# Fourier mixing with a gated convolution: the order of the first 55 microseconds changed on GpSimd, VectorE, ScalarE and TensorE

## The chip, the cores and the metric

The kernel runs on one core of a Trainium2 chip. A core has five engines with a queue of instructions each: TensorE (PE; its weight loads are PEld), VectorE (DVE), ScalarE (ACT), GpSimd (POOL) and SyncE (SP), which only starts transfers here. Within a queue the order is fixed when the program is built; between queues, semaphores carry the dependences. The metric is the time of one execution on the device, in microseconds.

## The reference

For each of 8 batches, `x` has 3136 positions and 256 features, all float32.

```python
X = np.fft.fft(x, axis=1); X = np.fft.fft(X, axis=2); x = X.real
h = np.maximum(x @ w_in, 0.0)                     # w_in 256 x 1024
conv_out[s] = conv_w[0]*h[s-1] + conv_w[1]*h[s] + conv_w[2]*h[s+1]   # zeros at both ends
out = (h * (1/(1+exp(-conv_out)))) @ w_out        # w_out 1024 x 256
```

The weights come as float64, each value in two 32-bit words, and have to be made float32 on the chip.

## The kernel before, in words

**Stages.** The transform along the sequence is folded by symmetry. Rows `x[s]` and `x[S-s]` are added and subtracted on VectorE (`xh`, then `w`), and TensorE multiplies the parts with tables of cosines and sines (`tab_109`, `tab_110`, 98 or 99 rows). This gives the two halves of the spectrum, `pt` and `qt`, in nine *units* for a batch: odd and even ones for both halves, and one called `feature`, which makes a single edge row (`pd`, then `er`). A unit has matmuls into a PSUM tile `po`, a `copy` of half of it to `as` on ScalarE, and a `fin` of sums and differences on VectorE that writes `pt` or `qt`. `part(0)` and `part(1)` are the two parts of an odd unit's matmuls. The tables are mirrored at run time on ScalarE (`mirror_even`, `mirror_tables`), and `mend_row` halves one row of them there.

The transform along the features is folded into the weights: TensorE multiplies `w_in` with a small table `dm` to give `G` (`blocks`, copied by ScalarE) and a column sum `ge` (`column`). So `w_in` has to be float32 first. It is converted in four quarters of two feature blocks each, `w_in[0]` to `w_in[3]`. Each of `w_in[1]` to `w_in[3]` takes five operations of VectorE and one of ScalarE: exponent (L653), a power of two from it (ScalarE, L655), mantissa (L667), lower word added (L668), sign (L661), product (L676). `w_out` follows by the same way.

**The main loop.** A batch is cut along the sequence in 4 *chunks*, each with 8 feature blocks of 128, which makes 32 *steps* a batch and 256 in all. Step s goes through these stages, at the cycles of the loop named in brackets, relative to its own: `seed` (ScalarE puts `eb` times `ge` in `pa`; -2), `products` (TensorE, into `pb` and `pa`; -1), `copies` (ScalarE, `nb` out of `pb`; -1), `combine` (VectorE, two custom instructions, `h` out of `pa` and `nb` with the relu; 0), `first_tap` (ScalarE, `g`; 0), `middle` (a transfer that adds the shifted `h` to `g`, started by GpSimd; 0), `last_tap` (VectorE; +3), `sigmoid` (ScalarE) and `gate` (VectorE; +4), and the product with `w_out` (TensorE; +5).

`row_of` takes an `h` tile for a step and has GpSimd set its two end columns to zero where the chunk asks for it (L820); `combine` of the step waits for that. In cycle t it is called for step t+1, ahead of `middle(t)`.

**What sets the order.** No scheduler: instructions stand on each queue in the order of the code. The loop has named places ("first", "act", "dve", "pool", "load", "pe"), and `at(cycle, place, f)` hangs extra work on one of them. With that the head of the program hands on what it has not done: the rest of the weights' conversion, `column` and `blocks` of the later quarters, and the loads for the next batch.

**The edge row.** `feature` writes the even entries of `er` on GpSimd (L459, L460). `flip` fetches the odd ones from the last partition of `qt` by a transfer on SP (L488), and GpSimd then negates every second of these (L489, the *sign change*). `store` writes `er` to a buffer in memory (`ed`, L492), and `spread` loads it back over all partitions, one tile `eb` for each chunk (L595). The first chunk's `eb` is not made in that way but in PSUM (`odd_first`, `even_first`, L981).

Of the kernel before, what the change touches and what calls it, by code (L numbers as in the profile page):

```python
# [10 lines left out]
I32 = mybir.dt.int32  # L11
U32 = mybir.dt.uint32
AF = mybir.ActivationFunctionType
# [24 lines left out]
def kernel(  # L38
# [100 lines left out]
    def fold_ops(b):  # L139
# [4 lines left out]
        def half(h):  # L144
# [65 lines left out]
            def scaled():  # L210
                if b == 0 and h:
                    a, c = sides()
                    for i, (v, k) in enumerate(((a, 0), (c, 2), (a, 1), (c, 0))):
                        if i % 2 == 0:
                            parted[h, i // 2] = hp.tile([P, HW], F32, name="h", tag="h")[:, 0:4 * P].rearrange(
                                "p (a s d) -> p a s d", a=2, s=2)
                        act(parted[h, i // 2][0:NP, i % 2], v, AF.Copy, scale=turn[0:NP, k, h:h + 1])
                    return
                made.append(rp.tile([P, 2, 2, P], F32, name="rt", tag="rt"))
                for i, v in enumerate(sides()):  # L220
                    act(made[0][0:NP, i], v, AF.Copy, scale=turn[0:NP, 1, h:h + 1])
# [84 lines left out]

    def mend_row(par, half):

        for st in range(2):
            row = tabs[0][96:NP, st, HQ - 1] if par == 0 else tabs[1][96:NP, st, 1]  # L310
            act(row, row, AF.Copy, scale=half[96:NP])

    def mirror_tables(h):

# [36 lines left out]
    def units(b):  # L351
# [134 lines left out]
        def flip():  # L486

            nc.sync.dma_start(out=er[b][:, 1:NK:2], in_=PQ[b][1][P - 1:P, 1:NK:2])  # L488
            nc.gpsimd.tensor_scalar(out=er[b][:, 3:NK:4], in0=er[b][:, 3:NK:4], scalar1=-1.0, scalar2=None, op0=ALU.mult)  # L489

        def store():
            nc.sync.dma_start(out=ed[b:b + 1, 0:NK], in_=er[b])  # L492

        return (begin, [odd_even(1), odd(1), even_even(1), even(1), feature(), odd_even(0), odd(0),
# [144 lines left out]
    def narrow(dst, raw, room=None):  # L639
# [7 lines left out]
        if room is not None:  # L647
            c, n = hi.shape[1:]
            sg = room[:, 0:c * n].rearrange("p (c n) -> p c n", c=c)

        def power():

            ts(out=d, in0=hi, scalar1=20, scalar2=0x7FF, op0=lsr, op1=ALU.bitwise_and)  # L653
            if room is not None:
                act(d, d, AF.Relu, scale=2.0 ** 23, bias=low[0:d.shape[0]])  # L655
            else:
                ts(out=d, in0=d, scalar1=-896, scalar2=0, op0=ALU.add, op1=ALU.max)
                ts(out=d, in0=d, scalar1=23, scalar2=None, op0=lsl)
# [1 line left out]
        def sign():  # L660
            stt(out=d, in0=hi, scalar=-0x80000000, in1=d, op0=ALU.bitwise_and, op1=ALU.bitwise_or)  # L661

        def product():

            if room is None:
                sign()
            ts(out=sg, in0=hi, scalar1=0xFFFFF, scalar2=0x100000, op0=ALU.bitwise_and, op1=ALU.bitwise_or)  # L667
            stt(out=lof, in0=lo.bitcast(U32), scalar=2.0 ** -32, in1=sg, op0=ALU.mult, op1=ALU.add)  # L668
            if room is None:
                value()  # L670

        def value():

            if room is not None:
                sign()
            stt(out=dst, in0=lof, scalar=2.0 ** -20, in1=dst, op0=ALU.mult, op1=ALU.mult)  # L676
        return (power, product) if room is None else (power, product, value)

    class Weight:

# [269 lines left out]
    mirror_tables(0)  # L950
    column(0)
    keep_on(1)
    mirror_even(0)
    mend_row(1, half)
    mirror_tables(1)
    folds(1)
    mirror_even(2)
    mend_row(0, half)
    mirror_even(1)
    mirror_even(3)  # L960
    room = left[:, NF // 2:].rearrange("p f i -> p (f i)").bitcast(I32)
    for f in load_ops(1, 0, nc.sync):
        f()
    for u in odds:
        u.part(0)
    for j, u in enumerate(odds):
        u.part(1)
        u.copy()
        u.fin()

    n = chunks[0].k1
    for i, u in enumerate(us[j] for j in (4, 2, 3, 7, 8)):
        u.matmuls(0, 1)
        if i == 0:
            p = spare()
            odd_first(p, n)
        u.copy()
        if i == 2:
            even_first(p, n)
            eb[0, 0] = ebp.tile([P, HN], F32, name="eb", tag="eb")[:, 0:n]  # L980
            nc.scalar.copy(out=eb[0, 0], in_=p[:, 0:n])  # L981
        u.fin()
    flip()
    store()
    spread(0, range(1, len(chunks)))
    steps = [(b, c, f) for b in range(B) for c in range(len(chunks)) for f in range(NF)]
    per = len(chunks) * NF
    side = {}
    taken = set()

# [2 lines left out]

    for i in (2, 3):
        at((0, 0, 1, 3)[i], "pe", lambda i=i: blocks(i))

    early, *rest = w_in[2].parts(0, 2, room)
    at(0, "first", lambda: column(1))
    at(0, "first", lambda: blocks(1))
    for fn in rest:  # L1000
        at(0, "dve", fn)
    for cycle, w_, c in ((1, w_in[3], 0), (3, w_out, 0), (5, w_out, 2), (7, w_out, 4), (9, w_out, 6)):
        for j, where, fn in zip((0, 0, 1), ("first", "dve", "dve"), w_.parts(c, c + 2, room)):
            at(cycle + j, where, fn)
    taken.update((0, 2, 4, 6, 8, 10))
    for j, fn in enumerate(load_ops(1, 1, nc.sync)):
# [67 lines left out]

    LAG = 5
    n = len(steps)
    row_of(steps[0])
    seed(steps[0])
    seed(steps[1])
    products(steps[0])  # L1080
    copies(steps[0])
    for f in w_in[1].parts(0, 2, room):
        f()
    early()
    for t in range(n + LAG):
        def run(where):
            for fn in side.get((t, where), []):
# [19 lines left out]
            last_tap(steps[t - 3])  # L1107
        if 0 <= t - 4 < n:
            gate(steps[t - 4])
        if t + 1 < n:  # L1110
            row_of(steps[t + 1])
        if t < n:
            middle(steps[t])
# [71 lines left out]
```

## Time and profile before

| what | us |
|---|---|
| median of 3 runs | 1160.87 |
| lowest and highest | 1160.75, 1161.49 |
| profiled execution | 1162.03 |
| its span | 1160.3 |
| PE busy in it | 1137.6 |
| DVE busy | 960.4 |
| ACT busy | 902.1 |
| POOL busy | 375.8 |

The granted clock of TensorE is 1.000 over the span. The span is what the trace covers; the rest of the execution lies around it. Times in the rows of the trace are microseconds from the start of the span. In a row there stand the start, the duration, the engine, the line of the kernel, the operation, the tile written and the tiles read, the shape, how many instructions the row groups, and in brackets the idle time of the engine ahead of it with what ended that. [...] PE is near full over the whole span, but not in the first 60 us, and it is these that the change touches.

### The profile page before, as it was taken

How to read it: one execution, taken by the hardware profiler on the slowest of the kernel's cores; microseconds unless marked ns; L12 is line 12 of the kernel's file. 1: busy time of each engine (PE TensorE's matmuls, PEld its weight loads, DVE VectorE, ACT ScalarE, POOL GpSimd, SP SyncE). 2: the span in 40 equal slices, each digit the busy share in tenths (PEclk: the TensorE clock that was granted, in tenths of full speed). 3: DMA queues.
4: the chain of work that ended last, by engine and by line, in shares of the span. 5: the costliest groups of instructions: out<-in, count | busy, mean ns of one | idle time of the engine just before them, and what ended most of it. 6: DMA issues, size and time to landing. Idle time of an engine off the chain costs nothing.

```text
span 1160.3 us, 15073 instructions
## 1 busy us (share of the span) xinstructions
PE 1137.6 (98%) x4824; PEld 887.2 (76%) x4824; DVE 960.4 (83%) x1452; ACT 902.1 (78%) x1709; POOL 375.8 (32%) x484
## 2 busy tenths in 40 slices
PE   6899999999999999999999999999999999999998
PEld 3667787778777877777777777778778777777777
DVE  8799889988988989798878879788886767877775
ACT  3688877878777878787877778887877777888884
POOL 6335523542343252425132331422121222122223
PEclk9999999999999999999999999999999999999999
DMA  9777985876757586756776766765664656666664
GB/s 251 162 109 178 169 159 125 182 167 152 164 120 168 119 198 143 169 114 154 147 171 128 153 140 122 177 129 120 142 128 93 125 118 138 139 131 129 123 118 100
DMA packets 107595, 167.49 MB, mean 144 GB/s; under 512 B 32104, under 2 KB 62838, under 8 KB 107517
## 3 DMA queue, kind: packets, MB, share of 16 engines
q0 software_dynamic: 42160, 115.87, 51.8%
q1 hardware_dynamic: 64616, 50.53, 15.8%
q8 instruction: 38, 0.62, 0.2%
q14 instruction: 40, 0.33, 0.1%
q10 hardware_dynamic: 741, 0.14, 0.1%
HBM read 37.80 MB, written 25.74 MB: 55 GB/s over the span
## 4 chain that ended last, share of the span: by engine, by line
PE 84%; DVE 5%; ACT 4%; issue 2%; POOL 1%; ACTq 0%; POOLq 0%; DVEq 0%
PE po L93 52%; PE pb L93 13%; PE pa L93 13%; PE pd L93 6%; DVE g L858 1%; ACT nb L835 1%; DVE g L885 1%; ACT os L913 1%; DVE h L843 1%; POOL xh L129 1%; ACT g L877 1%; ACT pa L814 0%; ACT g L849 0%; POOL w L176 0%; POOL g L853 0%
## 5 line engine op out<-in xcount | busy, mean ns | idle before, releaser
L93 PE MATMUL po<-wout,g 128*128 128x256 f32 x3072 | 706.3, 379 | 3.3 <-DVE g L885 3.2
L93 PEld LDWEIGHTS po<-wout,g 128*128 128x128 f32 x3072 | 580.6, 190 | 148.0 <-issue 17.6
L853 POOL DMA_DIRECT2D g<-h x256 | 219.7, 858 | 725.3 <-ACT g L849 453.1
L835 ACT ACTIVATE nb<-pb 128x386 f32<-128x386 f32 (+3 forms) x512 | 227.6, 499 | 167.4 <-PE pb L93 166.7
L843 DVE CUSTOM_DVE_ANT_0 h<-pa,nb 128x386 f32<-128x386 f32 (+3 forms) x512 | 265.0, 558 | 35.4 <-PE pa L93 22.6
L877 ACT ACTIVATE g<-g,cw 128x770 f32<-128x770 f32 (+3 forms) x264 | 246.1, 935 | 45.8 <-DVE g L858 44.4
L858 DVE SCALAR_TENSOR_TENSOR g<-h,cw,g 128x770 f32<-128x770 f32 (+1 forms) x256 | 265.4, 1037 | 0.3 <-DMA g<-h 0.3
L885 DVE TENSOR_TENSOR g<-g,h 128x770 f32<-128x770 f32 (+1 forms) x248 | 240.2, 968 | 22.4 <-ACT g L877 22.1
L849 ACT ACTIVATE g<-h,cw 128x770 f32<-128x770 f32 (+1 forms) x256 | 244.1, 953 | 0.0
L93 PE MATMUL pb<-qt,G 127*128 127x387 f32 (+2 forms) x512 | 213.8, 498 | 1.5 <-ACT nb L835 1.1
L93 PE MATMUL pa<-pt,G 128*128 128x387 f32 (+2 forms) x512 | 212.2, 495 | 1.4 <-ACT pa L814 1.3
L814 ACT ACTIVATE pa<-eb,ge 128x387 f32<-128x387 f32 (+2 forms) x256 | 155.3, 607 | 3.1 <-DVE h L843 1.4
L93 PEld LDWEIGHTS pa<-pt,G 128*128 128x128 f32 x512 | 96.5, 189 | 76.6 <-issue 19.2
L129 POOL DMA_INDIRECT xh<-in_x_dram,idx x64 | 97.7, 1527 | 20.2 <-issue 12.7
L93 PE MATMUL pd<-tab,w 98*128 98x197 f32 (+2 forms) x448 | 97.6, 317 | 0.0
L93 PEld LDWEIGHTS pb<-qt,G 127*128 127x128 f32 x512 | 90.9, 190 | 8.5 <-ACT nb L835 2.9
L93 PEld LDWEIGHTS pd<-tab,w 98*128 98x128 f32 (+1 forms) x448 | 82.0, 191 | 8.9
L913 ACT COPY os<-po 128x256 f32<-128x256 f32 x196 | 57.4, 392 | 6.3 <-PE po L93 6.3
L399 DVE TENSOR_TENSOR as<-as,pd 128x196 f32<-128x196 f32 x14 | 5.0, 358 | 46.0 <-ACT as L395 46.0
L176 POOL COPY w<-xh 98x4 f32<-98x4 f32 (+1 forms) x30 | 37.5, 1252 | 7.9 <-DVE xh L170 7.9
L154 DVE TENSOR_TENSOR xh<-xh 98x1020 f32<-98x1020 f32 (+1 forms) x32 | 38.6, 1210 | 0.4 <-DMA xh<-in_x_dram,idx 0.4
L165 DVE TENSOR_TENSOR xh<-xh 98x1024 f32<-98x1024 f32 (+1 forms) x32 | 38.9, 1214 | 0.1
(150 smaller groups left out, 430.4 us busy)
## 6 DMA issues: line engine op xcount, KB each, us to landing
g<-h POOLq DMA_DIRECT2D x192, 385.0 KB, 3.9
g<-h POOLq DMA_DIRECT2D x64, 416.0 KB, 4.2
out_dram<-os SPq DMA_DIRECT2D x96, 256.0 KB
xh<-in_x_dram SPq DMA_DIRECT2D x16, 784.0 KB
eb<-ed SPq DMA_DIRECT2D x16, 193.5 KB
raw<-in_moe_w_in_dram SPq DMA_DIRECT2D x4, 512.0 KB
raw<-in_moe_w_out_dram SPq DMA_DIRECT2D x1, 2048.0 KB
eb<-ed SPq DMA_DIRECT2D x8, 209.0 KB
```

The source lines that it names most:

```text
L93: nc.tensor.matmul(o, l, r, start=start, stop=stop, skip_group_check=True)
L129: nc.gpsimd.indirect_dma_start(out=xh[b, h][0:NP, 7 - m].rearrange("p q d -> p (q d)"), out_offset=None, in_=bass.AP(tensor=x.tensor, offs ...
L165: vt(flat(to, to + 2), flat(0, 2), flat(2, 4), op=op)
L814: act(pa[s][:, 0:n], eb[b, c], AF.Copy, scale=ge[:, f:f + 1])
L835: act(nb[s][:, i, cols], p[:, cols], AF.Copy, scale=-1.0 if i else 1.0)
L843: nc.vector._custom_dve(TENSOR_ADD_SAT, out=to, in0=a[:, cols], in1=c[:, i, cols], s0=BIG, s1=0.0)
L849: act(gs[s], hs[s][:, 0:n], AF.Copy, scale=cw[:, 0, s[2]:s[2] + 1])
L853: nc.gpsimd.dma_start(out=gs[s], in_=hs[s][:, 1:1 + n], accum_op=ALU.add)
L858: stt(out=g, in0=h[:, k:k + n], scalar=cw[:, k, f:f + 1], in1=g, op0=ALU.mult, op1=ALU.add)
L877: act(gs[s][:, c], gs[s][:, c], AF.Sigmoid, scale=cw[:, 1, s[2]:s[2] + 1])
L885: vt(g, g, h[:, 0:r.stop], op=ALU.mult)
L913: nc.scalar.copy(out=osb[:, j % 2], in_=pt[:, j % 2])
```

## The change

The change has three parts.

1. *Memsets and sign change.* `row_of` of steps 0 and 1 is called ahead of the loop, and in the loop for step t+1 from t = 1 on. The sign change moves out of `flip` into `store`, and `store` is hung on cycle 0's place "pool", behind `middle(0)`, with `spread` behind it. `flip`'s transfer is issued after the third of the last five units.
2. *Narrowing of `w_in[1]`.* `parts` gives six operations instead of two or three groups. For `w_in[1]` they are called apart: exponent and mantissa after the odd units, power after the copy of the first `eb`, lower after the third of the last five units, sign and value right ahead of the loop. The other quarters go in groups as before, through the new function `three`. Exponent and power of `w_in[2]` are called in cycle 0 ahead of `column(1)`, which is behind the `nb` copies of step 1.
3. *The head's ScalarE and TensorE work.* `mend_row` is one instruction over both halves of the table instead of two. The mirrors and the mending stand in another order: `mirror_even(2)` ahead of the scaled copies, and `mend_row(0)`, `mirror_even(1)` and `mirror_even(3)` between the copies of the odd units. Part 0 of all odd units comes first, in the order 0, 2, 1, 3. The four scaled copies of the turned parts stand in another order, and `odd_first` is called one unit later.

GpSimd before, from the last sum of the edge row to the second `middle` (`h` are the steps' tiles, `g<-h` is `middle`):

```order
L460 TENSOR_TENSOR er<-h 1x196
L489 TENSOR_SCALAR er<-er 1x392
L820 MEMSET h 128x2 x2
L853 DMA g<-h 128x770
L820 MEMSET h 128x2
L853 DMA g<-h 128x770
```

And now:

```order
L459 TENSOR_TENSOR er<-h 1x196
L825 MEMSET h 128x2 x2
L858 DMA g<-h 128x770
L490 TENSOR_SCALAR er<-er 1x392
L825 MEMSET h 128x2
L858 DMA g<-h 128x770
```

The first two memsets are ahead of the first `middle`, the sign change is behind it, and the memset of step 2 is behind the sign change.

VectorE before, from the end of `qt`'s even unit to combine(0) (L843; `win` and `raw` are `w_in[1]` and `left` is a scratch tile, the last L653 belongs to `w_in[2]`):

```order
L383 TENSOR_TENSOR qt<-po,as 128x392
L369 TENSOR_TENSOR as<-as,po 128x197
L371 TENSOR_TENSOR as<-as,po 128x196
L381 TENSOR_TENSOR pt<-as,po 128x393
L383 TENSOR_TENSOR pt<-as,po 128x392
L653 TENSOR_SCALAR win<-raw 128x512
L667 TENSOR_SCALAR left<-raw 128x512
L668 SCALAR_TENSOR_TENSOR raw<-raw,left 128x512
L661 SCALAR_TENSOR_TENSOR win<-raw,win 128x512
L676 SCALAR_TENSOR_TENSOR win<-raw,win 128x512
L653 TENSOR_SCALAR win<-raw 128x512
L843 ISA h<-pa,nb 128x385 x2
```

And now, from the end of the last odd unit on; behind it stand the product (L670), the exponent of `w_in[2]` (L651) and combine(0):

```order
L651 TENSOR_SCALAR win<-raw 128x512
L664 TENSOR_SCALAR left<-raw 128x512
L368 TENSOR_TENSOR as<-as,po 128x197
L370 TENSOR_TENSOR as<-po,as 128x196
L380 TENSOR_TENSOR qt<-as,po 128x393
L382 TENSOR_TENSOR qt<-po,as 128x392
L667 SCALAR_TENSOR_TENSOR raw<-raw,left 128x512
L368 TENSOR_TENSOR as<-as,po 128x197
L370 TENSOR_TENSOR as<-as,po 128x196
L380 TENSOR_TENSOR pt<-as,po 128x393
L382 TENSOR_TENSOR pt<-as,po 128x392
L661 SCALAR_TENSOR_TENSOR win<-raw,win 128x512
```

Two operations of the narrowing stand ahead of the even units' `fin`, one between them, two behind.

TensorE before, the end of the odd units and the start of `feature`:

```order
L93 MATMUL po<-tab_109,w 128x197 x2
L93 MATMUL po<-tab_110,w 128x196 x2
L93 MATMUL po<-tab_109,h 128x197 x4
L93 MATMUL po<-tab_110,w 128x196 x2
L93 MATMUL po<-tab_109,h 128x197 x4
L93 MATMUL pd<-tab_109,ea 1x197
```

And now:

```order
L93 MATMUL po<-tab_110,w 128x196 x4
L93 MATMUL po<-tab_109,w 128x197 x4
L93 MATMUL po<-tab_110,w 128x196 x4
L93 MATMUL po<-tab_109,h 128x197 x8
L93 MATMUL pd<-tab_109,ea 1x197
```

All matmuls with `tab_110` of the odd units' second round are ahead of the ones with `h`, the scaled copies.

```diff
--- before.py
+++ after.py
@@ -210,7 +210,7 @@
             def scaled():
                 if b == 0 and h:
                     a, c = sides()
-                    for i, (v, k) in enumerate(((a, 0), (c, 2), (a, 1), (c, 0))):
+                    for i, (v, k) in ((2, (a, 1)), (3, (c, 0)), (0, (a, 0)), (1, (c, 2))):
                         if i % 2 == 0:
                             parted[h, i // 2] = hp.tile([P, HW], F32, name="h", tag="h")[:, 0:4 * P].rearrange(
                                 "p (a s d) -> p a s d", a=2, s=2)
@@ -306,9 +306,8 @@
 
     def mend_row(par, half):
 
-        for st in range(2):
-            row = tabs[0][96:NP, st, HQ - 1] if par == 0 else tabs[1][96:NP, st, 1]
-            act(row, row, AF.Copy, scale=half[96:NP])
+        row = tabs[0][96:NP, 0:2, HQ - 1] if par == 0 else tabs[1][96:NP, 0:2, 1]
+        act(row, row, AF.Copy, scale=half[96:NP])
 
     def mirror_tables(h):
 
@@ -486,9 +485,9 @@
         def flip():
 
             nc.sync.dma_start(out=er[b][:, 1:NK:2], in_=PQ[b][1][P - 1:P, 1:NK:2])
+
+        def store():
             nc.gpsimd.tensor_scalar(out=er[b][:, 3:NK:4], in0=er[b][:, 3:NK:4], scalar1=-1.0, scalar2=None, op0=ALU.mult)
-
-        def store():
             nc.sync.dma_start(out=ed[b:b + 1, 0:NK], in_=er[b])
 
         return (begin, [odd_even(1), odd(1), even_even(1), even(1), feature(), odd_even(0), odd(0),
@@ -648,9 +647,10 @@
             c, n = hi.shape[1:]
             sg = room[:, 0:c * n].rearrange("p (c n) -> p c n", c=c)
 
+        def exponent():
+            ts(out=d, in0=hi, scalar1=20, scalar2=0x7FF, op0=lsr, op1=ALU.bitwise_and)
+
         def power():
-
-            ts(out=d, in0=hi, scalar1=20, scalar2=0x7FF, op0=lsr, op1=ALU.bitwise_and)
             if room is not None:
                 act(d, d, AF.Relu, scale=2.0 ** 23, bias=low[0:d.shape[0]])
             else:
@@ -660,21 +660,26 @@
         def sign():
             stt(out=d, in0=hi, scalar=-0x80000000, in1=d, op0=ALU.bitwise_and, op1=ALU.bitwise_or)
 
-        def product():
-
-            if room is None:
-                sign()
+        def mantissa():
             ts(out=sg, in0=hi, scalar1=0xFFFFF, scalar2=0x100000, op0=ALU.bitwise_and, op1=ALU.bitwise_or)
+
+        def lower():
             stt(out=lof, in0=lo.bitcast(U32), scalar=2.0 ** -32, in1=sg, op0=ALU.mult, op1=ALU.add)
-            if room is None:
-                value()
 
         def value():
-
-            if room is not None:
-                sign()
             stt(out=dst, in0=lof, scalar=2.0 ** -20, in1=dst, op0=ALU.mult, op1=ALU.mult)
-        return (power, product) if room is None else (power, product, value)
+        if room is None:
+            return exponent, power, sign, mantissa, lower, value
+        return exponent, power, mantissa, lower, sign, value
+
+    def three(ops):
+
+        def run(i, j):
+            def f():
+                for g in ops[i:j]:
+                    g()
+            return f
+        return run(0, 2), run(2, 4), run(4, 6)
 
     class Weight:
 
@@ -950,28 +955,39 @@
     mirror_tables(0)
     column(0)
     keep_on(1)
+    mend_row(1, half)
     mirror_even(0)
-    mend_row(1, half)
     mirror_tables(1)
+    pres[len(ops) - 4] = lambda f=pres[len(ops) - 4]: (mirror_even(2), f())
     folds(1)
-    mirror_even(2)
-    mend_row(0, half)
-    mirror_even(1)
-    mirror_even(3)
-    room = left[:, NF // 2:].rearrange("p f i -> p (f i)").bitcast(I32)
     for f in load_ops(1, 0, nc.sync):
         f()
-    for u in odds:
+    room = left[:, NF // 2:].rearrange("p f i -> p (f i)").bitcast(I32)
+    exponent, power, mantissa, lower, sign, value = w_in[1].parts(0, 2, room)
+    for u in odds[::2] + odds[1::2]:
         u.part(0)
-    for j, u in enumerate(odds):
+    for u in odds[::2]:
         u.part(1)
-        u.copy()
-        u.fin()
+    odds[0].copy()
+    odds[0].fin()
+    mend_row(0, half)
+    odds[1].part(1)
+    odds[1].copy()
+    odds[1].fin()
+    mirror_even(1)
+    odds[2].copy()
+    odds[2].fin()
+    mirror_even(3)
+    odds[3].part(1)
+    odds[3].copy()
+    odds[3].fin()
+    exponent()
+    mantissa()
 
     n = chunks[0].k1
     for i, u in enumerate(us[j] for j in (4, 2, 3, 7, 8)):
         u.matmuls(0, 1)
-        if i == 0:
+        if i == 1:
             p = spare()
             odd_first(p, n)
         u.copy()
@@ -979,12 +995,15 @@
             even_first(p, n)
             eb[0, 0] = ebp.tile([P, HN], F32, name="eb", tag="eb")[:, 0:n]
             nc.scalar.copy(out=eb[0, 0], in_=p[:, 0:n])
+            power()
         u.fin()
-    flip()
-    store()
-    spread(0, range(1, len(chunks)))
+        if i == 2:
+            flip()
+            lower()
     steps = [(b, c, f) for b in range(B) for c in range(len(chunks)) for f in range(NF)]
     per = len(chunks) * NF
+    for i in range(2):
+        row_of(steps[i])
     side = {}
     taken = set()
 
@@ -993,14 +1012,17 @@
 
     for i in (2, 3):
         at((0, 0, 1, 3)[i], "pe", lambda i=i: blocks(i))
-
-    early, *rest = w_in[2].parts(0, 2, room)
+    at(0, "pool", store)
+    at(0, "load", lambda: spread(0, range(1, len(chunks))))
+
+    early, *rest = three(w_in[2].parts(0, 2, room))
+    at(0, "first", early)
     at(0, "first", lambda: column(1))
     at(0, "first", lambda: blocks(1))
     for fn in rest:
         at(0, "dve", fn)
     for cycle, w_, c in ((1, w_in[3], 0), (3, w_out, 0), (5, w_out, 2), (7, w_out, 4), (9, w_out, 6)):
-        for j, where, fn in zip((0, 0, 1), ("first", "dve", "dve"), w_.parts(c, c + 2, room)):
+        for j, where, fn in zip((0, 0, 1), ("first", "dve", "dve"), three(w_.parts(c, c + 2, room))):
             at(cycle + j, where, fn)
     taken.update((0, 2, 4, 6, 8, 10))
     for j, fn in enumerate(load_ops(1, 1, nc.sync)):
@@ -1074,14 +1096,12 @@
 
     LAG = 5
     n = len(steps)
-    row_of(steps[0])
     seed(steps[0])
     seed(steps[1])
     products(steps[0])
     copies(steps[0])
-    for f in w_in[1].parts(0, 2, room):
-        f()
-    early()
+    sign()
+    value()
     for t in range(n + LAG):
         def run(where):
             for fn in side.get((t, where), []):
@@ -1107,7 +1127,7 @@
             last_tap(steps[t - 3])
         if 0 <= t - 4 < n:
             gate(steps[t - 4])
-        if t + 1 < n:
+        if 1 <= t < n - 1:
             row_of(steps[t + 1])
         if t < n:
             middle(steps[t])
```

## The prediction

> **What bounds the kernel now.** I read the table by windows first, to see where VectorE or TensorE is full; then the waits before the loop is under way; then the rows of each engine there. The whole difference between the two programs lies in the first 55 us. From combine(2) on, every engine has the same rows in the same order.
>
> In the table by windows the columns are the window, its length, and then the busy time of each engine, PE, PEld, DVE, ACT, POOL:
>
> ```profile
> 29.00:46.20 17.20, 16.08 (x101) 12.66 (x99) 10.73 (x27) 9.58 (x28) 8.52 (x12) 1.00 0.70 175
> 46.20:60.00 13.80, 11.50 (x48) 7.53 (x48) 13.59 (x26) 11.93 (x26) 4.06 (x8) 1.00 0.77 144
> 60.00:80.00 20.00, 19.63 (x77) 14.27 (x78) 19.83 (x34) 17.71 (x31) 6.33 (x14) 1.00 0.80 117
> 80.00:100.00 20.00, 18.48 (x74) 13.25 (x73) 19.96 (x30) 17.26 (x48) 8.50 (x6) 1.00 0.76 168
> 120.00:140.00 20.00, 20.00 (x85) 15.69 (x84) 16.31 (x24) 17.43 (x34) 12.61 (x11) 1.00 0.96 192
> ```
>
> VectorE (DVE) is full from 46.2 to 100 (13.59 of 13.80, 19.83 and 19.96 of 20.00), then TensorE takes over (20.00 of 20.00 in 120 to 140). Ahead of 46.2 VectorE works only 10.73 of 17.20 us. So what the head can give is VectorE time in which nothing runs. The waits, with total, count and longest:
>
> ```profile
> POOL er L489 <- DMA er<-qt: 6.8, 1, 6.8
> DVE h L843 <- POOL h L820: 2.8, 1, 2.8
> DVE as L399 <- ACT as L395: 1.9, 1, 1.9
> PE po L93 <- DVE g L885: 3.2, 7, 1.1
> ```
>
> GpSimd (POOL) sits 6.8 us at the sign change, waiting for the transfer that brings `er`; the memsets of the first `h` tiles stand behind it, and combine(0) on VectorE waits 2.8 us for them. The fourth row is TensorE's largest wait after 46 us: it is for VectorE's gate, so TensorE follows VectorE there and a shift of VectorE passes through to it.
>
> VectorE's rows (start, duration, line, tile, then idle time before and who ended it):
>
> ```profile
> 30.93 0.36 DVE L399 TENSOR_TENSOR as<-as,po 128x196 f32<-128x196 f32 x1 [1.93 <-ACT as L395]
> 34.82 0.56 DVE L431 TENSOR_TENSOR pt<-as 128x392 f32<-128x392 f32 x1
> 36.09 0.36 DVE L369 TENSOR_TENSOR as<-as,po 128x197 f32<-128x197 f32 x1 [0.71 <-ACT as L365]
> 38.20 0.36 DVE L369 TENSOR_TENSOR as<-as,po 128x197 f32<-128x197 f32 x1 [0.34 <-ACT as L365]
> 39.28 0.57 DVE L381 TENSOR_TENSOR pt<-as,po 128x393 f32<-128x393 f32 x1 [0.45 <-PE po L93]
> 40.23 0.42 DVE L653 TENSOR_SCALAR win<-raw 128x512 int32<-128x512 int32 x1
> 42.35 0.69 DVE L676 SCALAR_TENSOR_TENSOR win<-raw,win 128x512 f32<-128x512 f32 x1
> 42.96 0.42 DVE L653 TENSOR_SCALAR win<-raw 128x512 int32<-128x512 int32 x1
> 46.18 1.02 DVE L843 CUSTOM_DVE_ANT_0 h<-pa,nb 128x385 f32<-128x385 f32 x2 [2.81 <-POOL h L820]
> 51.89 1.02 DVE L843 CUSTOM_DVE_ANT_0 h<-pa,nb 128x385 f32<-128x385 f32 x2
> ```
>
> Its idle time here is 1.93 + 0.71 + 0.34 + 0.45 + 2.81 = 6.24 us, none of it between combine(0) at 46.18 and combine(2) at 51.89. The work of VectorE ahead of combine(2) is the same set of instructions in both programs. Therefore the gain is the start of combine(2) before, 51.89, less its start after, provided VectorE runs on without a new wait.
>
> **The change part by part.** GpSimd's rows carry the first part:
>
> ```profile
> 34.89 0.89 POOL L459 TENSOR_TENSOR er<-h 1x197 f32<-1x197 f32 x1
> 36.23 0.60 POOL L459 TENSOR_TENSOR er<-h 1x196 f32<-1x196 f32 x1
> 44.17 1.96 POOL L489 TENSOR_SCALAR er<-er 1x392 f32<-1x392 f32 x1 [6.77 <-DMA er<-qt]
> 46.00 0.14 POOL L820 MEMSET h<- 128x2 f32 x2
> 49.06 1.01 POOL L853 DMA_DIRECT2D g<-h  x1 [2.92 <-ACT g L849]
> 49.74 0.45 POOL L820 MEMSET h<- 128x2 f32 x1
> ```
>
> *Memsets.* The two memsets now follow the last L460, which ends before 38, long before combine(0) and combine(1). The wait of 2.81 is gone. What comes late next is the narrowing of `w_in[1]`. VectorE finished it at 42.35 + 0.69 = 43.04. Two of its five operations (2 x 0.42) and `lower` (0.69) now lie between the units, in waits for them (0.71, 0.34, 0.45), and the even units come 0.83 earlier by the next part: 43.04 - 0.84 - 0.69 - 0.83 = 40.7. After the next `exponent` (0.42) combine(0) starts at about 41.1.
>
> *The sign change goes behind middle(0), and step 2's memset now stands behind the sign change.* This is a new wait: combine(2) can't start before that memset, that waits for the sign change, that for middle(0)'s issue, and that for first_tap(0) on ScalarE. So I need the time of first_tap(0), which hangs on TensorE and ScalarE:
>
> ```profile
> 24.02 3.09 PE L93 MATMUL po<-tab,w 98*128 98x197 f32 x16 [0.33 <-ACT tab L269]
> 28.18 1.66 PE L93 MATMUL po<-tab,h 98*128 98x197 f32 x8 [1.07 <-ACT tab L269]
> 29.68 0.83 PE L93 MATMUL po<-tab,w 99*128 99x196 f32 x4
> 31.84 0.88 PE L93 MATMUL pd<-tab,ea 99*1 99x197 f32 x16
> 39.08 0.81 PE L93 MATMUL pb<-qt,G 127*128 127x386 f32 x2
> 43.09 1.05 PE L93 MATMUL po<-dm,win 128*128 128x1 f32 x8 [0.68 <-DVE win L676]
> 27.77 0.61 ACT L269 ACTIVATE tab<-tab 99x196 f32<-99x196 f32 x2
> 28.41 1.13 ACT L311 ACTIVATE tab<-tab,half 2x393 f32<-2x393 f32 x2
> 46.02 0.37 ACT L787 COPY G<-po 128x256 f32<-128x256 f32 x1 [0.49 <-PE po L93]
> 47.30 0.59 ACT L814 ACTIVATE pa<-eb,ge 128x386 f32<-128x386 f32 x1 [0.91 <-DVE h L843]
> 47.83 0.92 ACT L849 ACTIVATE g<-h,cw 128x770 f32<-128x770 f32 x1
> 48.65 0.85 ACT L835 ACTIVATE nb<-pb 128x385 f32<-128x385 f32 x2
> ```
>
> *TensorE and ScalarE order.* The four matmuls of 29.68 (0.83) are moved ahead of the `po<-tab,h` ones, into the wait of 1.07, so `pd` starts at 31.84 - 0.83 = 31.0. Its bounds: 1.07 earlier, if the gap goes altogether (30.8), and no earlier at all (31.84), if the merged mend (two of 1.13 together; one over twice the width, I take 0.9 to 1.13) and the mirrors, which now stand between the copies, hold it. From `pd` to `pb` TensorE has no wait in either order, 39.08 - 31.84 = 7.24, so `pb` goes from 39.08 to 38.25.
>
> *The chain to combine(2).* Each step is a difference of two starts in the rows above.
> - From `pb` to the column matmuls of `w_in[1]`: 43.09 - 39.08 = 4.01, less the wait of 0.68 for the narrowing, which ends earlier now: 3.33, at 41.6.
> - To the end of the second `G` copy: 46.02 + 0.37 - 43.09 = 3.30, at 44.9.
> - Seed and first tap: 47.83 + 0.92 - 47.30 = 1.45, at 46.3 (combine(0) is done by 42.2, so the wait of 0.91 goes).
> - To middle(0)'s issue: 49.06 - 48.75 = 0.31; to the next instruction of GpSimd: 49.74 - 49.06 = 0.68. The sign change starts at 47.3.
> - Sign change to memset: 46.00 - 44.17 = 1.83; memset to combine: 46.18 - 46.00 = 0.18. combine(2) starts at 49.3. (With a memset of 0.45 as at 49.74 in place of 0.14, at 49.6.)
>
> Gain: 51.89 - 49.3 = 2.6. Of the 6.24 idle some 3.6 remain, the larger part now in front of combine(2): VectorE, from 41.1 on, has 51.89 - 46.18 = 5.7 of work ahead of it and would be ready at 46.8. The bounds: `pd` at 30.8 gives 2.8, the slower memset 2.3, both `pd` at 31.84 and the slower memset 1.5.
>
> *What costs nothing.* The store of `ed` and the three loads of `eb` come some 3 us later on SP (46.16 before). They are wanted by the seed of chunk 1:
>
> ```profile
> 47.48 1.30 SPq L595 DMA_DIRECT2D eb<-ed  x3
> 66.66 0.59 ACT L814 ACTIVATE pa<-eb,ge 128x387 f32<-128x387 f32 x1
> ```
>
> That leaves 19 us before and 16 or more after. Behind them on SP stand only table loads. `power` of `w_in[2]` now follows the `nb` copies of step 1 (0.85) on ScalarE, but its product is wanted only in the cycle after. The scaled copies in another order, and the odd units' two rounds, change who waits inside the 17 us that the `pd` term already counts.
>
> [...] The first L459 took 0.89 beside VectorE's L431 at 34.82, the second 0.60: 0.29 more. [...]
>
> **The rivals.**
> - *The memset doesn't hold combine(2)*, because the sign change is much shorter or the work on VectorE much later. For it: 1.96 is long for 392 elements of one partition beside 0.60 for 196. Against: it was measured beside an idle VectorE, with nothing to delay it. Then `nb` of step 2 sets the start: 46.3 + 0.85 = 47.1, a gain of 4.8, 1156.1.
> [...]
> - *The gain is lost on the way*: VectorE has no slack until 100, but TensorE's own queue (19.63 of 20.00 in 60 to 80) may set the end already. Then 1160.9, no change. Against it stand TensorE's 3.2 us of waits for VectorE.
> - *Slower: the `er` transfer comes late.* It took from its issue to 44.17 before, and now step 2's memset, all later middles and the memsets stand behind it on GpSimd. combine(2) is then the landing plus 1.83 + 0.18 = 2.0; it equals before's 51.89 at a landing of 49.9, 5.7 later than 44.17. At 52.5 it would start at 54.5, 2.6 later: 1163.5. For it: it queued behind larger loads. Against: its issue and those ahead of it on SP stand in the same order.
>
> **How the numbers follow.** The profiled execution took 1162.03 (span 1160.3), 1.2 above the median of 1160.87. The sum is a difference inside that span, so I take it off the median: 1160.87 - 2.6 = 1158.3. A measurement of this kernel can tell about 0.2%, 2.3 us, from no change. Chances: the forecast 0.65 (gain 1.5 to 2.9, of which I put 0.46 above 2.3 and 0.19 below), no hold 0.10, ports 0.12, lost 0.06, slower 0.07. Faster: 0.46 + 0.10 = 0.56; same: 0.19 + 0.12 + 0.06 = 0.37; slower 0.07. The range leaves out the slower case and the far half of the no-hold case: from a gain of 4.3 (1156.6) to one of 0.5 (1160.4).
>
> **What would show it.** In the profile after: no wait of combine(0) for a memset; `pd` at about 31.0 and `pb` at about 38.2; the sign change at about 47.3, started by the end of middle(0)'s issue and not by the `er` transfer; a wait of some 2.5 us before combine(2), for L825's memset; combine(2) near 49.3, then VectorE full to 100. The prediction is wrong if combine(2) starts elsewhere, if VectorE has further waits behind it, or if the time doesn't follow combine(2).

## The result, and the profile after

The changed kernel takes 1159.16 us (median of 20 runs, 1158.59 to 1159.77), the kernel before 1161.32 in the runs beside it (1160.26 to 1162.96). The ratio is 0.9981, with a 95% interval from 0.9974 to 0.9988: 2.2 us less, clear of the scatter but at the edge of the 0.2% that I had set as the bound. The forecast was 2.6 less. A second set of runs of the same kernel on another occasion gave 1159.31, 0.9984 [0.9975, 0.9993], which is 1.6 less than before's 1160.90 beside it.

The profiled execution took 1159.72 (span 1157.9). In the table by windows, with the columns as before, the two windows that change:

```profile
29.00:46.20 17.20, 16.13 (x99) 12.79 (x100) 14.91 (x36) 10.27 (x28) 7.28 (x11) 1.00 0.71 184
46.20:60.00 13.80, 12.28 (x54) 8.33 (x53) 11.47 (x21) 13.51 (x29) 6.79 (x11) 1.00 0.76 165
```

VectorE works 14.91 us in the first window, 4.2 more than before, and 11.47 in the second, 2.1 less: a wait has gone from the first and a new one stands in the second. The waits of the head:

```profile
POOL g L858 <- ACT g L854: 13.5, 3, 8.8
DVE h L848 <- POOL h L825: 2.2, 1, 2.2
PE po L93 <- ACT tab L310: 0.9, 1, 0.9
```

GpSimd no longer waits for `er`. VectorE waits for a memset again, now step 2's, and TensorE has a wait for the mending (L310) that it did not have. The rows of VectorE, GpSimd, TensorE and ScalarE behind these numbers:

```profile
40.82 0.69 DVE L670 SCALAR_TENSOR_TENSOR win<-raw,win 128x512 f32<-128x512 f32 x1
41.77 1.01 DVE L848 CUSTOM_DVE_ANT_0 h<-pa,nb 128x385 f32<-128x385 f32 x2
46.81 0.71 DVE L667 SCALAR_TENSOR_TENSOR raw<-raw,left 128x512 f32<-128x512 uint32 x1
49.70 1.02 DVE L848 CUSTOM_DVE_ANT_0 h<-pa,nb 128x385 f32<-128x385 f32 x2 [2.19 <-POOL h L825]
38.01 0.13 POOL L825 MEMSET h<- 128x2 f32 x2
46.97 0.99 POOL L858 DMA_DIRECT2D g<-h  x1 [8.84 <-ACT g L854]
47.67 1.98 POOL L490 TENSOR_SCALAR er<-er 1x392 f32<-1x392 f32 x1
49.52 0.14 POOL L825 MEMSET h<- 128x2 f32 x1
29.33 2.37 PE L93 MATMUL po<-tab,h 98*128 98x197 f32 x12 [0.87 <-ACT tab L310]
31.88 0.88 PE L93 MATMUL pd<-tab,ea 99*1 99x197 f32 x16 [0.18 <-issue]
38.95 0.81 PE L93 MATMUL pb<-qt,G 127*128 127x386 f32 x2
42.13 0.95 PE L93 MATMUL po<-dm,win 128*128 128x1 f32 x8
24.35 0.62 ACT L269 ACTIVATE tab<-tab 99x196 f32<-99x196 f32 x2 [0.69 <-DMA tab<-dft_seq_dram]
28.33 0.94 ACT L310 ACTIVATE tab<-tab,half 2x786 f32<-2x786 f32 x1
```

combine(0) starts at 41.77 instead of 46.18, four microseconds and more earlier. But combine(2) waits 2.19 for the memset behind the sign change and starts at 49.70 instead of 51.89, 2.19 earlier. From there VectorE runs on as before: combine(3) and combine(4) start 2.2 earlier too, and the span is 2.4 shorter. So the chain that the forecast built, from first tap over middle(0) and the sign change to the memset, is the one that holds. One thing does not fit: `pd` starts at 31.88, where it was at 31.84, although the forecast took 0.83 off. Two experiments go after that.

### The profile page after: what moved, and what is told of

It reads as the page before. It is cut to its first block, busy times and chain, and to the rows that moved or that the text cites. A ratio compares the mean times of both kernels' runs of the same rounds, so it can differ in the third digit from the quotient of the medians.

```text
span 1157.9 us, 15068 instructions
## 1 busy us (share of the span) xinstructions
PE 1137.4 (98%) x4824; PEld 887.7 (77%) x4824; DVE 960.3 (83%) x1452; ACT 901.4 (78%) x1707; POOL 376.3 (32%) x484
## 4 chain that ended last, share of the span: by engine, by line
PE 85%; DVE 5%; ACT 5%; issue 2%; POOL 2%; DMA 1%; SPq 0%; ACTq 0%; POOLq 0%; DVEq 0%
PE po L93 53%; PE pb L93 13%; PE pa L93 13%; PE pd L93 6%; DVE g L863 1%; DVE g L890 1%; ACT os L918 1%; ACT nb L840 1%; POOL xh L129 1%; DMA xh<-in_x_dram 1%; DVE h L848 1%; ACT pa L819 1%; ACT g L882 0%; ACT g L854 0%; DMA tab<-dft_seq_dram 0%
```

## The experiments

Theory 1 was the forecast's: the hold in front of combine(2) is the price that is left, and what lies behind follows it. The rival was that TensorE and ScalarE are close behind and set the pace as soon as the hold is shorter.

**Take the hold away.** A third memset goes ahead of the loop.

```diff
-    for i in range(2):
+    for i in range(3):
         row_of(steps[i])
...
-        if 1 <= t < n - 1:
+        if 2 <= t < n - 1:
             row_of(steps[t + 1])
```

> The changed kernel with a third memset (step 2's) ahead of the loop, so that it no longer stands behind the sign change. Theory 1 (the hold in front of combine(2) is the price, everything behind it follows it): the wait of 2.19 goes, combine(2) starts at about 47.5, where VectorE and nb of step 2 are ready in the trace of after, and the time is 2.2 below after's 1159.2: 1157.0. Rival (TensorE and ScalarE are right behind): TensorE has no gap from 45.4 to 50.2 in after, nb of step 3 is ready at 51.1 whatever GpSimd does, so combine(3) can come only 1.2 earlier than its 52.31, and the time is 1158.0. Second rival (nothing in the head reaches the end): 1159.2.

Measured: 1158.06, 0.9971 [0.9960, 0.9982] of before; 1.1 below the changed kernel. The rival's number. VectorE's rows of that run, combine(2) and combine(3):

```profile
47.27 1.02 DVE L848 CUSTOM_DVE_ANT_0 h<-pa,nb 128x385 f32<-128x385 f32 x2
50.88 1.03 DVE L848 CUSTOM_DVE_ANT_0 h<-pa,nb 128x385 f32<-128x385 f32 x2 [0.84 <-PE pa L93]
```

combine(2) comes without a wait at 47.27, 2.4 earlier, but combine(3) then waits 0.84 for TensorE's `pa` of step 3 and is only 1.4 earlier. So the hold of 2.19 is worth 1.1 in time; the rest lies over TensorE's chain. With the hold gone, the time follows combine(3) and no longer combine(2).

**Make the hold longer.** The sign change of batch 0 is done three times over (a factor of -1 each time, so the value is the same).

```diff
-            nc.gpsimd.tensor_scalar(out=er[b][:, 3:NK:4], ...)
+            for _ in range(3 if b == 0 else 1):
+                nc.gpsimd.tensor_scalar(out=er[b][:, 3:NK:4], ...)
```

> The changed kernel with the sign change of batch 0 done three times over. If step 2's memset behind it sets combine(2) and all that follows, the two extra ones cost 2 x 1.85 in full: combine(2) at 53.4 for the table landing of after, the wait in front of it 5.9 instead of 2.19, and 1162.9, slower than the kernel before. If the hold is covered by TensorE's chain in part, combine(3) has 1.2 to give: 1161.7.

Measured: 1163.35, 1.0020 [1.0011, 1.0029] of before and 4.0 above the changed kernel in the same set of runs (1159.31). That is the full price, and more than the 3.7 expected, because the two extra ones took 3.97 (the row has 5.95 for the three, against 1.98 for the one).

```profile
46.96 5.95 POOL L491 TENSOR_SCALAR er<-er 1x392 f32<-1x392 f32 x3
52.97 1.02 DVE L849 CUSTOM_DVE_ANT_0 h<-pa,nb 128x385 f32<-128x385 f32 x2 [6.17 <-POOL h L826]
```

The wait in front of combine(2) is 6.17 instead of 2.19. Together: a longer hold costs all of itself, and taking the hold away gives 1.1. This is also how near the change stands to a loss: two more sign changes on that queue, and it is slower than before.

**The parts one by one.** First the memsets and the moved sign change alone, put into the kernel before (of the first part of the change all but the earlier place of `flip`'s transfer, nothing else):

> The kernel before with the first part alone (memsets ahead, sign change and store behind the first middle). Worked out from the rows of before: combine(0) right behind VectorE's L653 at about 43.4, second G copy still at 46.4, first tap ends 47.9, middle 48.2, sign change 48.9, combine(2) about 50.9, so 1.0 below before's 1161.3: 1160.3. Rival (the first part is the whole change): 1159.2.

Measured: 1161.6, 1.0001 [0.9992, 1.0010]. No gain, 1.3 above what was expected. Yet its profile shows combine(2) where the expectation had it:

```profile
23.45 0.62 ACT L269 ACTIVATE tab<-tab 99x196 f32<-99x196 f32 x2 [0.91 <-DMA tab<-dft_seq_dram]
50.75 0.56 DVE L843 CUSTOM_DVE_ANT_0 h<-pa,nb 128x385 f32<-128x385 f32 x1 [1.87 <-POOL h L820]
```

50.75 against 51.89 before. That profiled execution (1160.86) was the fastest of the eleven of its kernel, while the profile of before (1162.03) was 0.7 slower than that kernel's median. A difference of two such profiles isn't the difference of the medians. What moves them comes further down.

Then the narrowing alone, in the kernel before:

> The kernel before with the second part alone (w_in[1] narrowed between the unit sums). Theory 1: combine(0) still waits for the memset behind the sign change and starts at 46.2, and VectorE's 5.7 us to combine(2) stand behind it: no change, 1161.3, with a longer wait at combine(0), some 4.5 instead of 2.8. Rival (TensorE and ScalarE set the pace): the column matmuls come about 0.8 earlier and with them the end: 1160.5.

Measured: 1160.7 in the median, with a ratio of 1.0001 [0.9991, 1.0011]: no change that can be told, as expected. The median by itself lies nearer to the rival's 1160.5; two of the eleven executions, 1163.83 (the profiled one) and 1166.11, bring the ratio up. So the time doesn't decide between the two, but the row of combine(0) does:

```profile
46.80 1.02 DVE L849 CUSTOM_DVE_ANT_0 h<-pa,nb 128x385 f32<-128x385 f32 x2 [3.98 <-POOL h L826]
```

combine(0) waited 3.98 for the memset (4.5 was expected) and started 1.99 behind the sign change at 44.81, as in the kernel before. What VectorE had saved went into that wait. The wait is 1.17 longer than before, and 0.6 of that is only that `er` landed later than in the first profile of before.

Then the changed kernel without its third part (mending in two instructions; mirrors, scaled copies, odd units and `odd_first` in the order of before):

> The changed kernel with the third part undone (two-instruction mending, mirrors, scaled copies, odd units and odd_first in the order of before). By the prediction's step the feature matmuls (pd) go back by 0.83 and combine(2) with them: 1160.0. By the trace of after, in which pd starts at 31.88 against 31.84 before, the third part is worth 0.1: 1159.3.

Measured: 1160.51, 0.9995 [0.9986, 1.0004]; 1.35 above the changed kernel. So the third part is worth something, more than the forecast's 0.83, though `pd` seemed not to have moved at all. Its rows (ScalarE's first mirror of `tab_109`, then `pd`, then combine(3)) solve it:

```profile
23.55 0.62 ACT L269 ACTIVATE tab<-tab 99x196 f32<-99x196 f32 x2 [0.27 <-DMA tab<-dft_seq_dram]
31.77 0.53 PE L93 MATMUL pd<-tab,ea 99*1 99x197 f32 x8
52.45 1.01 DVE L849 CUSTOM_DVE_ANT_0 h<-pa,nb 128x385 f32<-128x385 f32 x2
```

The first L269 waits for the transfer of the tables, and in this execution that landed 0.8 earlier (23.55) than in the profile of after (24.35). Counted from the landing, `pd` comes 31.77 - 23.55 = 8.22 later here, and 31.88 - 24.35 = 7.53 later with the third part; in before it was 31.84 - 23.61 = 8.23. The reordering takes 0.70 off this stretch, and the later landing hid it when I laid one trace beside the other. All profiles of these kernels agree: `pd` stands 8.22 to 8.24 behind the landing in the seven without the third part, and 7.52 or 7.53 in the four that have it unaltered. The median's 1.35 is more than these rows give; that rest is not explained.

**Two transfers land at another time in each run.** So I took second and third profiles of the kernels as they are.

> The kernel before, unchanged, for a second profile. Theory (two transfers land at another time in each execution, and each kernel hangs on one of them: before on the odd entries of er, the changed kernel on the tables): here too combine(0) starts 2.0 behind the landing of er, the span moves with that landing and not with ScalarE's first L269 (the tables), and a span near the median of 1159.6 goes with a landing some 0.7 earlier than the 44.17 of the first profile. Rival (the runs differ by something behind the head): combine(0) at 46.2 again and another span.

> The kernel before, unchanged, for a third profile. Theory: combine(0) starts about 2.0 to 2.2 behind the start of the sign change, and combine(3) 8.3 behind combine(0), wherever the tables land, so the span is 1160.3 less (46.18 minus combine(0)) unless the clock drops on the way.

> The changed kernel, unchanged, for a second profile and its time on the same chip as the next ones. Theory: the stretch from the table landing (ScalarE's first L269) to pd is 7.5 again and to combine(3) 28.0, so the span moves with that landing: 1157.9 less (24.35 minus the landing). The er transfer does not matter: the sign change starts 0.7 behind middle(0). Median 1159.2, as before. Rival (the landing does not carry through): the same span at another landing.

The kernel before, second profile:

```profile
23.65 0.62 ACT L269 ACTIVATE tab<-tab 99x196 f32<-99x196 f32 x2 [1.22 <-DMA tab<-dft_seq_dram]
43.05 2.18 POOL L489 TENSOR_SCALAR er<-er 1x392 f32<-1x392 f32 x1 [5.66 <-DMA er<-qt]
45.28 1.03 DVE L843 CUSTOM_DVE_ANT_0 h<-pa,nb 128x385 f32<-128x385 f32 x2 [1.87 <-POOL h L820]
```

and third:

```profile
23.67 0.62 ACT L269 ACTIVATE tab<-tab 99x196 f32<-99x196 f32 x2 [1.01 <-DMA tab<-dft_seq_dram]
44.02 1.96 POOL L489 TENSOR_SCALAR er<-er 1x392 f32<-1x392 f32 x1 [6.50 <-DMA er<-qt]
46.04 1.02 DVE L843 CUSTOM_DVE_ANT_0 h<-pa,nb 128x385 f32<-128x385 f32 x2 [2.61 <-POOL h L820]
```

The tables landed at nearly the same time in all three (23.61, 23.65, 23.67), and the transfer of `er` was issued at the same time (33.25, 33.24, 33.25). The sign change, which starts when `er` is in, started at 44.17, 43.05 and 44.02, combine(0) at 46.18, 45.28 and 46.04 (2.0 to 2.2 behind it), and the spans were 1160.3, 1159.4 and 1160.1, which is combine(0) plus 1114.1 each time. The changed kernel, second profile, for which a span of 1157.9 - (24.35 - 23.80) = 1157.35 was to be expected:

```profile
23.80 0.62 ACT L269 ACTIVATE tab<-tab 99x196 f32<-99x196 f32 x2 [0.52 <-DMA tab<-dft_seq_dram]
31.32 0.87 PE L93 MATMUL pd<-tab,ea 99*1 99x197 f32 x16 [0.19 <-issue]
49.13 1.02 DVE L848 CUSTOM_DVE_ANT_0 h<-pa,nb 128x385 f32<-128x385 f32 x2 [2.19 <-POOL h L825]
51.73 1.02 DVE L848 CUSTOM_DVE_ANT_0 h<-pa,nb 128x385 f32<-128x385 f32 x2
```

Its span was 1157.4. `pd` stands 7.52 behind the landing (7.53 in the first profile), combine(3) 27.93 (27.96). So the kernel before hangs on the landing of `er`, and the changed kernel on that of the tables. That is probably also why the first part alone showed no gain: it exchanges one landing for the other, with a hold of 1.87 in front of combine(2). It is not shown, since this kernel has one profile only, and in it the tables landed earliest of all fourteen profiles (23.45; the others 23.54 to 24.35). Nor do the landings on record say what is typical for `er`: in the kernels that wait for it, the sign change started at 42.15, 43.05, 44.02, 44.17 and 44.81.

One thing holds in all fourteen profiles: the span is 1105.5 to 1105.8 more than the start of combine(3), from 1155.0 and 49.47 in the fastest kernel here to 1160.3 and 54.48 in the first profile of before. So what makes these kernels differ lies ahead of combine(3).

From the landing of the tables to combine(3) the parts add up: 29.90 with the first alone (53.35 - 23.45), 28.90 with the second added (52.45 - 23.55), 27.96 with all three. In medians: 1161.6, 1160.51, 1159.16, in steps of 1.1 and 1.35 where the rows have 1.00 and 0.94.

**The memsets alone.** The kernel before with three memsets ahead of the sign change, which stays in its place:

```diff
+    steps = [(b, c, f) for b in range(B) for c in range(len(chunks)) for f in range(NF)]
+    for i in range(3):
+        row_of(steps[i])
     flip()
     store()
...
-    row_of(steps[0])
     seed(steps[0])
...
-        if t + 1 < n:
+        if 2 <= t < n - 1:
             row_of(steps[t + 1])
```

> The kernel before with nothing but three memsets put ahead of the sign change, which stays where it was, waits for er, and has no combine behind it. Theory: combine(0) at about 43.1 as in the run with the first part alone, no hold in front of combine(2), combine(3) when TensorE's pa of step 3 is done, 51.8 against 53.35 there: 1.5 below that run's 1161.6, 1160.1. Rival (the sign change has to be moved for the gain): 1161.4.

Measured: 1159.78, 0.9991 [0.9982, 1.0000] of before, with an interval that ends at no change. The run with the first part alone was 0.2 above the before beside it (1161.4), this one is 1.3 below its own (1161.07): 1.5 between them, as expected. By the times, then, the memset behind the sign change had eaten the first part's gain, and three moved memsets, with nothing else, bring about half of what the whole change brings (1.3 of 2.2 in the medians, 0.0009 of 0.0019 in the ratios).

The rows of the one profile don't show it. The eleven executions fall into two groups, seven from 1159.08 to 1159.79 and four from 1160.61 to 1161.57, and the profiled one is the slowest. In it combine(0) is at 44.28 (43.1 expected) and combine(3) at 53.99 (51.8 expected):

```profile
42.15 1.92 POOL L489 TENSOR_SCALAR er<-er 1x392 f32<-1x392 f32 x1 [4.60 <-DMA er<-qt]
42.30 1.26 DVE L676 SCALAR_TENSOR_TENSOR win<-raw,win 128x512 f32<-128x512 f32 x1
43.48 0.87 DVE L653 TENSOR_SCALAR win<-raw 128x512 int32<-128x512 int32 x1
43.61 1.05 PE L93 MATMUL po<-dm,win 128*128 128x1 f32 x8 [1.24 <-DVE win L676]
44.28 1.00 DVE L843 CUSTOM_DVE_ANT_0 h<-pa,nb 128x385 f32<-128x385 f32 x2
53.99 1.02 DVE L843 CUSTOM_DVE_ANT_0 h<-pa,nb 128x385 f32<-128x385 f32 x2 [1.23 <-PE pa L93]
```

`er` landed early, so the sign change on GpSimd ran beside VectorE's narrowing, and there VectorE's product took 1.26 instead of 0.69 and the exponent behind it 0.87 instead of 0.42 (42.35 and 42.96 in before). TensorE waited 1.24 for the product, where it had waited 0.68. A sign change that stays in its place can thus meet VectorE when `er` is early; behind `middle(0)` it comes later. Whether the other three of the upper group are of this kind is not known; their mean clock was 1.000, and 0.998 in the profiled one. For a median execution (span 1158.0) combine(3) would be at 52.2, an estimate by the 1105.8 above.

**The mending on GpSimd.** TensorE's new wait of 0.87 is for `mend_row(0)` on ScalarE. Here GpSimd does it, ahead of the odd units:

```diff
-        act(row, row, AF.Copy, scale=half[96:NP])
+        if par == 0:
+            nc.gpsimd.tensor_scalar(out=row, in0=row, scalar1=half[96:NP], ...)
+        else:
+            act(row, row, AF.Copy, scale=half[96:NP])
...
     mirror_even(0)
+    mend_row(0, half)
     mirror_tables(1)
...
     odds[0].fin()
-    mend_row(0, half)
```

> The changed kernel with mend_row(0) taken from ScalarE to GpSimd, which is idle there, and ahead of the odd units. By the trace of after TensorE waits 0.87 for this mending at 29.33, and has no wait from there to pb, so pd, pb and combine(2) come 0.8 earlier: 1158.4. From the table landing (ScalarE's first L269) to pd it is 7.53 in after; expected 6.7 here. Rival (ScalarE's mirrors between the copies hold pd instead): 7.3 or more, 1159.0.

Measured: 1158.9, 0.9982 [0.9973, 0.9991]; it can't be told from the changed kernel. The rival was right: `pd` stands 7.38 behind the landing (30.94 - 23.56).

```profile
27.35 2.97 PE L93 MATMUL po<-tab,h 98*128 98x197 f32 x16
30.94 0.87 PE L93 MATMUL pd<-tab,ea 99*1 99x197 f32 x16 [0.62 <-issue]
30.25 0.32 ACT L397 COPY as<-po 128x196 f32<-128x196 f32 x1 [0.45 <-DVE as L403]
30.47 0.62 ACT L269 ACTIVATE tab<-tab 99x196 f32<-99x196 f32 x2
```

The sixteen matmuls have no wait left, but TensorE is idle for 0.62 in front of `pd`, while the last mirror (L269 at 30.47) stands behind a copy that waits 0.45 for VectorE. One wait went, the next took its place. The row names no engine as the cause; that it is the mirror is read from the order, and the last run tests it.

**Put together.** Mending on GpSimd with the third memset, then also both mirrors ahead of the third odd copy:

```diff
     mirror_even(1)
+    mirror_even(3)
     odds[2].copy()
     odds[2].fin()
-    mirror_even(3)
```

> The third memset ahead and mend_row(0) on GpSimd together. If TensorE's chain sets the pace once the hold is gone, both gains add: 1.1 of the memset and 0.8 of the mending below after's 1159.2, 1157.3. If VectorE does, the mending adds nothing: 1158.1.

> The run with the mending on GpSimd and three memsets, with mirror_even(3) ahead of the third odd copy as well. There pd waited for the second mirror on ScalarE (TensorE idle 0.6 in front of pd), which stood behind a copy that waited 0.46 for VectorE. pd then starts 0.4 earlier, 6.8 behind the table landing instead of 7.2, and with TensorE's chain setting the pace the time is 0.4 lower: 1157.2. If something else sets it: 1157.6.

Measured: 1157.56, 0.9971 [0.9959, 0.9982], and 1157.07, 0.9960 [0.9946, 0.9973]. The last is the fastest here, 2.2 below the changed kernel in the same set of runs. In it `pd` follows the matmuls with nothing between them:

```profile
24.61 2.99 PE L93 MATMUL po<-tab,w 98*128 98x197 f32 x16 [0.17 <-ACT tab L269]
27.43 2.96 PE L93 MATMUL po<-tab,h 98*128 98x197 f32 x16
30.32 0.88 PE L93 MATMUL pd<-tab,ea 99*1 99x197 f32 x16
```

`pd` was forecast 0.4 earlier than with the single mirror ahead (30.74 in that run), and it is. But that is partly luck: the tables landed later (24.19 against 23.54), and counted from there `pd` comes after 6.13, where 6.8 was expected. With the 0.17 in the first row as its only wait since 22.01, TensorE's own work sets `pd` in this run, and no longer the landing.

Whether the two gains add can't be told from the times: the ratio of both together is 0.9971, the same as that of the three memsets alone. It can be told from the rows. combine(3) stands 19.14 or 19.15 behind `pd` in all three kernels without the hold (50.88 - 31.74, 49.88 - 30.74, 49.47 - 30.32), and 20.41 to 20.43 in the changed kernel and in the one with the mending on GpSimd alone. So the hold costs 1.3 in the rows, and what TensorE gains ahead of `pd` reaches combine(3) in full. The sum of 1157.3 was missed by 0.3; the mending had been put in with 0.8, and the way from the landing to `pd` got only 0.33 shorter (7.20 against 7.53).

## Why the prediction was right

**The direction and the mechanism** were right. combine(0) no longer waits for a memset; the wait of 2.81 came back as one of 2.19 (2.5 forecast) behind the sign change; combine(0) started at 41.77 (41.1 forecast) and combine(2) at 49.70 (49.3 forecast); VectorE ran on from there; the time followed combine(2). That it followed combine(2) holds because of the new wait: with that taken away, it follows combine(3) and TensorE.

**The chain** was right step by step. From `pb` to combine(2) it was 49.70 - 38.95 = 10.75, where the forecast had 49.3 - 38.25 = 11.05. The sign change took 1.98 (1.96 in the row used), the memset 0.14, as in the lower of its two bounds.

**The step on TensorE's order** was mis-sized and met a wait that I had only in its bounds. The four matmuls did fill the gap, but twelve of the sixteen matmuls behind them (by the trace's count; the program's order has eight) then waited 0.87 for the mending. From the landing of the tables the step measures 0.70, not 0.83. In the two traces it measures nothing, since the tables landed 0.74 later in the second. The forecast took `pd` as a fixed time of the span, where it stood 8.22 to 8.24 behind the landing of a transfer without the third part and 7.52 or 7.53 with it.

**The gain of 2.6** was 0.4 too large against 2.2. By the second set of runs (1.6) it was 1.0 too large; the interval of the first has room for it. The sum started from a profiled execution of before that was 0.7 above its median; the profile of after had its own late landing, so the difference of the two profiles (2.19 at combine(2)) comes out near that of the medians by chance. The other pairs of profiles of the two kernels give 1.3 to 2.8. The text took the sum as a difference inside one span and moved it to the median as it was; that is the step that lacked a term.

**The rivals.** *No hold* did not come about. With the hold taken away, combine(2) does start where this rival had it (47.27, 47.1 forecast), but its gain of 4.8 was too high: it is 3.3, since combine(3) then waits for TensorE. *Ports*, with 0.12 among the chances: no run shows a port, only how long instructions took. The sign change was no longer than before (1.98 against 1.96), with VectorE waiting beside it. In other runs VectorE worked beside it. With the hold taken away, VectorE's sign operation starts in the middle of the sign change on GpSimd:

```profile
47.52 1.99 POOL L490 TENSOR_SCALAR er<-er 1x392 f32<-1x392 f32 x1
48.20 0.77 DVE L661 SCALAR_TENSOR_TENSOR win<-raw,win 128x512 int32<-128x512 int32 x1
```

It took 0.77, where it took 0.68 in the profile of after, with 1.3 of the sign change left to run. In the run with the memsets alone the product took 1.26 instead of 0.69, with 1.8 left. So VectorE lost 0.09 and 0.57 there, both less than what was left of the sign change.

*Lost on the way*: no. *Late `er`*: the sign change starts 0.70 after middle(0)'s issue in both profiles (at 47.67 and 47.11), so `er` had landed by then, and the landings seen in the kernels that wait for it (42.15 to 44.81) end 2 us and more short of mattering.

**What costs nothing** cost nothing, but with less to spare: the loads of `eb` started at 51.13 and the seed of chunk 1 at 64.53, which leaves 13 us instead of the 16 or more of the text. And behind these loads on SP stand not only table loads but three from `x` too (L545 before), which started at 57.17 instead of 52.61.

## What to carry to other kernels

In a head that waits for transfers, find for each kernel the landing that its chain starts from, and count from there: two profiles laid side by side by the clock of the span can hide 0.7 us or invent it. When a slow instruction is moved behind something on the same queue, look at what stands behind it next, here a memset of 0.14 us with VectorE waiting for it; moving the small thing instead of the slow one gave about half the gain (1.3 of 2.2 us). And price the removal of a wait by the next chain behind it, not by its length: 2.19 us of wait were worth 1.1. Where that chain takes over, the place to count from moves as well, here from combine(2) to combine(3).

## What was not expected

In three of the fourteen profiles TensorE's granted clock dropped for some microseconds between 44 and 60, each time behind a stretch in which TensorE had been partly idle. Two windows and the slowed matmuls of the run with the memsets alone, then two windows of the run with three sign changes:

```profile
40.00:44.00 4.00, 2.76 (x10) 1.28 (x10) 3.93 (x7) 1.37 (x3) 1.85 (x1) 1.00 0.25 42
44.00:48.00 4.00, 3.67 (x14) 2.54 (x14) 3.93 (x9) 2.20 (x7) 0.07 (x1) 0.65 0.19 58
44.53 3.14 PE L93 MATMUL po<-win,dm 128*128 128x256 f32 x8
50.00:54.00 4.00, 1.06 (x3) 0.30 (x2) 1.03 (x3) 0.41 (x2) 3.47 (x5) 1.00 0.00 2
56.00:60.00 4.00, 4.00 (x18) 3.39 (x17) 3.97 (x8) 2.98 (x8) 1.93 (x4) 0.68 0.73 209
```

In the first, TensorE was busy 2.76 of 4 us, and in the next four the clock was 0.65. The eight `po` matmuls took 3.14 there, against 1.97 in the profiles of before and after, which puts 1.2 us into the head. The third case is the profile with the narrowing alone: TensorE busy 1.73 of 3.80 us from 46.2 to 50, then a clock of 0.57 from 50 to 54. In the run with three sign changes, where the longer hold leaves TensorE busy for 1.06 of 4 us, the drop seems to come in most executions: the mean clock over the span was 0.998 or less in eight of the eleven, where all eleven of the changed kernel beside it have 0.999 or 1.000. Whether the idle time is the cause is not shown: no run changed it alone, and the profile of after has TensorE busy only 2.95 of 4 us from 28 to 32 and a clock of 1.00 there and from 32 to 36.

The mending took 0.94 on ScalarE as one instruction, where two took 1.13, and 3.30 on GpSimd. It cost nothing there, since GpSimd's next instruction waited 3.62 for VectorE all the same.
